# A list scheduler whose machine model is replaced, with 243 instead of 225 score tiles on VectorE

## The chip, the cores and the metric

The kernel runs on one core of one Trainium2 chip. Its engines are TensorE (PE, with its weight loads listed apart as PEld), VectorE (DVE), ScalarE (ACT), GpSimd (POOL) and SyncE (SP). The metric is the device time of one execution in microseconds. The kernel before took 881.84 us, the median of three runs (879.56 to 889.25). One further execution, which took 881.67 us, was recorded by the hardware profiler; all views of the profile are from it.

## The reference

Two attention branches read the same input and are mixed by a gate. All operands are bfloat16; S = 2048 tokens, D = 512, H = 32 heads of 16.

```python
g = sigmoid((x * gate_w).sum(-1, keepdims=True))
# branch A: softmax attention
q, k, v = split(x @ A_wqkv)                     # 32 heads of 16
p = softmax(q @ k.T / 4)                        # 2048 x 2048 for each head
a = (p @ v) @ A_wo
# branch B: linear attention with softmax features
q, k, v = split(x @ B_wqkv)
phi = lambda t: concat(softmax(t @ w_phi), softmax(-t @ w_phi))
num = phi(q) @ (phi(k).T @ v);  den = phi(q) @ phi(k).sum(0)
b = (num / (den + 1e-6)) @ B_wo
out = g * a + (1 - g) * b
```

Nearly all the work is branch A's 32 x 2048 x 2048 exponentials and the two products around them.

## The kernel before

**Tiles.** A score tile is 128 keys by 512 queries of one head: 32 heads x 16 key tiles x 4 query chunks = 2048 tiles. Four heads that share a quarter-wise layout go together, so the tiles are numbered in packs of four (512 packs); an output group is 16 packs (all key tiles of four heads and one query chunk), and there are 32 groups. A score matmul (`_scores`, L792) contracts over 32 rows (two heads of 16, the other head's queries set to zero), and stands in one of four row groups of the array ("row" kind). A value matmul (`_values`, L893) has 32 output columns (the head's 16 values, a column of ones that gives the softmax's sum, and 15 that nobody reads) and stands in one of four column groups ("col" kind). Everything else on TensorE uses the full array ("full" kind).

**Who computes the exponential.** ScalarE takes most tiles. PSUM has eight banks; five form a ring for ScalarE's scores, which are taken in groups of three and two banks in turn: `_qk` issues two or three score matmuls (L792), `_exp` one ACTIVATE over 1536 or 1024 columns (L837) into the SBUF ring ET. The score group k waits for the exponential k - 2, whose banks it reuses. The remaining three banks serve all else. VectorE takes the tiles named in `self.away`: `SHARES` gives for each output group how many of its 64 tiles go there, 225 in all. They are worked in batches of five (`_vector_batch`): a score matmul "vqk" for each into a common bank (also L792), its evacuation to integers (L731), and then on all five together four polynomial steps (L740, L742, L744, L746) and a last one (L748) that makes the bits of a bfloat16 exponential, in tile vu. The value product of such a tile is "pvx", also at L893, which reads vu.

**Filling TensorE.** `_fill` (L900) adds four matmuls with zero weights to the open output bank, one for each column group, which change nothing in the sum but keep the array busy. While no output bank is open (between the last value product of a group and the first of the next), `_qk` can put up to two full matmuls ahead of its scores into a bank that these overwrite (L809, called pads here).

**Other work.** The projections of branch A run ahead of the heads that need them (L582 for K and Q, L640 for V), the query halves are spread by small DMAs from SP (L624), the outputs are transposed and normalised on VectorE (`_norm`: L914 to L930), branch B (`_branch_b`) is put between, with 16 ScalarE exponentials of 2048 columns (L1057), and output projections close each query chunk (L1171 and L1204).

**What sets the order.** Every operation is recorded as an `Op` in `Plan` with its engine, a cost in microseconds, dependencies, a due time (`prio`) and a release position (`rel`). `Plan.order` is a list scheduler: it keeps for each engine the time at which it is free, takes the operation that can start first, and among those that start within 0.02 us the one with the lowest due time. The outcome is a fixed instruction order for each engine; on the chip the engines run these orders and meet at semaphores (`emit`, `_waits`), so the planner's times themselves do not reach the chip. Four parts of this model matter here:

- costs: `c_act`, `c_dve` and constants in the calls; VectorE's are lowered by 0.06 when placed, and `LAT` is added between dependent operations (on VectorE also within the engine);
- TensorE as one resource with a single free time, a cost for each operation and `SWITCH` where the kind changes;
- a limit for other TensorE work while a score group is available, from the 51st score group on: its ready time plus the cost of the exponential that runs, less `AHEAD` = 0.7;
- fills and pads, added where the array's share of the last 3 us is low (`SHARE`, `PAD`).

Constants place the rest: `LEAD`, `VPRIO` and `VREL` say how far ahead VectorE's batches are due, `QDUE` the query projections, `TPRIO` the transposes of finished outputs, `KEEP` the pack from which a bank is reserved for the next output group, `K0`, `SK`, `Q0` and `SQ` branch B.

Of the kernel before, what the change touches and what calls it, by code (L numbers as in the profile page):

```python
# [7 lines left out]
ALU = mybir.AluOpType  # L8
# [32 lines left out]
class Op:  # L41
    def __init__(self, eng, fn, cost, name, prio, rel, kind, lat):
        self.eng, self.fn, self.cost, self.name = eng, fn, cost, name
        self.prio, self.rel, self.kind, self.lat = prio, rel, kind, lat
        self.deps = []
# [16 lines left out]
class Plan:  # L62
# [4 lines left out]
    LAT = {"PE": 0.20, "ACT": 0.16, "DVE": 0.08, "POOL": 0.12, "SP": 2.2}  # L67
    SWITCH = 0.12
    SPAN, SHARE, FILL = 3.0, 0.6, 0.2133
    PAD, PADS, OVER = 0.5, 2, 0.3  # L70
# [9 lines left out]
    def op(self, eng, fn, cost, reads=(), writes=(), deps=(), name="", prio=0.0, rel=-99, kind="full",  # L80
           acquire=None, release=None, lat=None, array=None):
        o = Op(eng, fn, cost, name, prio, rel, kind, self.LAT[eng] if lat is None else lat)
# [27 lines left out]

    def order(self):
# [9 lines left out]
        last_kind = None  # L121
# [3 lines left out]
        seq = {id(o): i for i, o in enumerate(self.ops)}  # L125
        while left:
            best = None
            for e in self.ENGS:
                found, limit = [], 1e9
                for o in avail[e]:  # L130
# [3 lines left out]
                    t = free[e]  # L134
                    for d in o.deps:
                        r = d.end + (d.lat if d.eng != e or e != "PE" else 0.0)
                        if r > t:
                            t = r
                    if o.acquire is not None:
                        if not self._bank_for(o):  # L140
                            continue
                        r = min(b[1] for b in self.free_banks)
                        if r > t:
                            t = r
                    o.ready = t
                    found.append(o)
                    if o.slack is not None:
                        limit = min(limit, t + o.slack)
                for o in found:
                    cost = o.cost + (self.SWITCH if o.kind != last_kind else 0.0)  # L150
                    o.fits = o.slack is not None or o.ready + cost <= limit
                    key = (o.ready, o.prio, seq[id(o)])
                    if o.fits and (best is None or key < best[0]):
                        best = (key, e)
# [7 lines left out]
            for o in avail[e]:  # L162
                if not o.fits:
                    continue
                if o.ready <= t0 + 0.02:
                    key = (o.prio, seq[id(o)])
# [4 lines left out]
            t = max(o.ready, free[e])  # L171
            while e == "PE" and self.open is not None and self.pad:
                f = free["PE"]
                x = Op("PE", self.pad(self.open), self.FILL, "pad", o.prio, -99, "col", 0.2)
                x.start, x.end = f, f + self.FILL + self.SWITCH * (last_kind != "col")
                room = t + self.OVER * (o.kind == "col") - x.end
                have = sum(r[1] for r in recent if r[0] > f - self.SPAN)
                if have >= self.SHARE * self.SPAN or room < 0:
                    break
                last_kind = "col"  # L180
                free["PE"] = x.end
                recent.append((x.start, self.FILL))
                x.array = self.FILL
                queues["PE"].append(x)
            t = max(t, free[e])
            cost = o.cost - (0.06 if e == "DVE" else 0.0)
            if e == "PE" and o.kind != last_kind:
                cost += self.SWITCH
                last_kind = o.kind
            if e == "PE":  # L190
                recent = [r for r in recent if r[0] > t - self.SPAN]
                recent.append((t, o.array))
                low = lambda share: sum(r[1] for r in recent) < share * self.SPAN
                while o.filler > o.filled and low(self.SHARE) or (
                        o.pad and self.open is None and o.filled < self.PADS and low(self.PAD)):
                    o.filled += 1
                    cost += self.FILL
                    recent.append((t, self.FILL))
            o.start, o.end = t, t + cost
            free[e] = o.end  # L200
# [11 lines left out]
            for u in o.users:  # L212
                u.left -= 1
                if not u.left:
                    avail[u.eng].append(u)
# [85 lines left out]
class _Kernel:  # L301
# [5 lines left out]
    AHEAD = 0.7  # L307
    NB, NVU, LEAD = 5, 3, 17
    QDUE, VPRIO, VREL, TPRIO = 20.0, -4.0, 27.0, 11.0
    KEEP = 14  # L310
# [91 lines left out]
    def c_act(n):  # L402
        return 0.089 + n * 0.000812

    @staticmethod
    def c_dve(n):
        return 0.16 + n * 0.00105

    @staticmethod
    def c_pe(n):  # L410
        return 0.004 + n * 0.000417
# [134 lines left out]
    def _x_transpose(self, j, half, bank=None):  # L546
# [4 lines left out]
        for t2 in range(2):  # L551
# [13 lines left out]
            self._bank(job).bitcast(BF16).rearrange("p (t c q) -> p t c q", t=2, c=4)), 0.7,  # L565
# [65 lines left out]
    def _proj_v(self, cp, j):  # L631
# [5 lines left out]
        for tt in range(4):  # L637
# [6 lines left out]
            mm = op("PE", run, 4 * 0.09, reads=[self.b_xT[j], self.b_WA[2][cp > 0]], deps=[mm], name="vproj", prio=due,  # L644
# [6 lines left out]
    def _gate(self):  # L651
# [5 lines left out]
        for qc in range(NQC):  # L657
            job = Job()

            def mm(e, qc=qc, job=job):  # L660
# [8 lines left out]
                self.T1[:, k].rearrange("p b d -> p (b d)"), self._bank(job)), 0.74, deps=[m], name="gate_t",  # L669
# [14 lines left out]
        for j in range(4):  # L684
# [6 lines left out]
    SHARES = (0, 0, 2, 6, 5, 5, 7, 7, 8, 8, 8, 6, 8, 7, 9, 8,  # L691
              10, 6, 8, 7, 8, 7, 8, 6, 9, 8, 9, 6, 8, 9, 11, 11)
# [22 lines left out]
    def _vector_batch(self, number, units, due, step):  # L715
# [10 lines left out]
        for j, u in enumerate(units):  # L726
# [3 lines left out]
                   acquire=job, array=0.0533)  # L730
# [10 lines left out]
           0.16 + n * 0.00053, reads=[b_vt], writes=[b_vf], name="v_frac", prio=prio)  # L741
        op("DVE", lambda e: e.tensor_scalar(flat(vu), flat(vf), CUBE, SQUARE, op0=ALU.mult, op1=ALU.add),  # L742
           0.16 + n * 0.00027, reads=[b_vf], writes=[b_vu], name="v_line", prio=prio)
        op("DVE", lambda e: e.tensor_tensor(flat(vf), flat(vf), flat(vf), ALU.mult), 0.16 + n * 0.00053,  # L744
# [516 lines left out]
```

## Time and profile before

| | |
|---|---|
| three runs | 879.56, 881.84, 889.25 us |
| the profiled execution | 881.67 us |
| its span, first to last instruction | 879.9 us |
| ScalarE busy | 858.1 us (98%) |
| TensorE busy | 819.6 us (93%) |
| VectorE busy | 774.5 us (88%) |
| mean granted TensorE clock | 0.994 |

The span is the time from the first to the last instruction; 1.77 us of the execution lie around it. Busy time of an engine is the union of its instructions' records. A record lasts longer than the engine's spacing between two instructions, because an instruction drains while the next one runs; so the busy time of ScalarE and VectorE contains short waits. Matmul ends are modelled, so TensorE's busy time is an upper figure as well.

### The profile page before, as it was taken

How to read it: one execution, taken by the hardware profiler on the slowest of the kernel's cores; microseconds unless marked ns; L12 is line 12 of the kernel's file. 1: busy time of each engine (PE TensorE's matmuls, PEld its weight loads, DVE VectorE, ACT ScalarE, POOL GpSimd, SP SyncE). 2: the span in 40 equal slices, each digit the busy share in tenths (PEclk: the TensorE clock that was granted, in tenths of full speed). 3: DMA queues.
4: the chain of work that ended last, by engine and by line, in shares of the span. 5: the costliest groups of instructions: out<-in, count | busy, mean ns of one | idle time of the engine just before them, and what ended most of it. 6: DMA issues, size and time to landing. Idle time of an engine off the chain costs nothing.

```text
span 879.9 us, 17614 instructions
## 1 busy us (share of the span) xinstructions
PE 819.6 (93%) x7777; PEld 253.6 (29%) x7777; DVE 774.5 (88%) x1040; ACT 858.1 (98%) x749; POOL 7.3 (1%) x14
## 2 busy tenths in 40 slices
PE   8999999999999999998989989999999999999998
PEld 3333223223222222222223222232322322232222
DVE  4469588898999989899898997989999999899996
ACT  5999999999999999999999999999999999999996
POOL 3000000000000000000000000000000000000000
PEclk9999999999999989999999999999999999999999
DMA  7200000000000000000000000000000000000000
GB/s 240 55 2 1 7 1 3 6 1 7 1 7 2 7 1 1 8 1 7 1 1 8 1 7 19 7 7 1 13 14 9 6 1 7 19 7 8 1 1 25
DMA packets 14700, 11.51 MB, mean 13 GB/s; under 512 B 5536, under 2 KB 14112, under 8 KB 14624
## 3 DMA queue, kind: packets, MB, share of 16 engines
q1 hardware_dynamic: 12752, 9.73, 3.8%
q8 instruction: 61, 1.00, 0.5%
q10 hardware_dynamic: 1872, 0.66, 0.3%
q14 instruction: 15, 0.12, 0.1%
HBM read 6.31 MB, written 2.10 MB: 10 GB/s over the span
## 4 chain that ended last, share of the span: by engine, by line
ACT 88%; PE 8%; DVE 2%; DMA 1%; SPq 0%; issue 0%; ACTq 0%
ACT ET L837 85%; ACT bq L1057 3%; PE ps L792 3%; PE ps L893 1%; PE ps L900 1%; DVE WB L1005 1%; DMA WA<-in_A_wqkv_dram 1%; PE ps L809 1%; PE ps L582 1%; SPq L624 0%; PE ps L662 0%; DMA qT<-qraw 0%; PE ps L1204 0%; PE ps L1171 0%; DVE kT L605 0%
## 5 line engine op out<-in xcount | busy, mean ns | idle before, releaser
L837 ACT ACTIVATE ET<-ps 128x1536 bf16<-128x1536 f32 x729 | 831.6, 1398 | 12.5 <-PE ps L792 11.8
L792 PE MATMUL ps<-qT,kT 32*128 32x512 bf16 x2048 | 332.5, 386 | 47.9 <-ACT ET L837 37.5
L900 PE MATMUL ps<-kT,zero 128*32 128x512 bf16 x2352 | 224.0, 386 | 0.0
L893 PE MATMUL ps<-ET,V 128*32 128x512 bf16 x1823 | 204.5, 385 | 0.0
L792 PEld LDWEIGHTS ps<-qT,kT 32*128 32x128 bf16 x2048 | 81.4, 91 | 351.4 <-ACT ET L837 293.6
L731 DVE TENSOR_SCALAR vt<-ps 128x512 uint32<-128x512 f32 x225 | 150.1, 683 | 28.2 <-PE ps L792 26.8
L748 DVE SCALAR_TENSOR_TENSOR vu<-vt,vu 128x2560 int16<-128x2560 uint32 x45 | 126.7, 2816 | 0.4
L893 PE MATMUL ps<-vu,V 128*32 128x512 bf16 x225 | 86.1, 386 | 0.0
L900 PEld LDWEIGHTS ps<-kT,zero 128*32 128x32 bf16 x2352 | 54.6, 94 | 73.8 <-issue 60.6
L893 PEld LDWEIGHTS ps<-ET,V 128*32 128x32 bf16 x1823 | 54.8, 95 | 64.0 <-issue 42.4
L740 DVE TENSOR_SCALAR vf<-vt 128x2560 f16<-128x2560 uint8 x45 | 66.8, 1485 | 0.2
L744 DVE TENSOR_TENSOR vf<-vf 128x2560 f16<-128x2560 f16 x45 | 66.7, 1481 | 0.3
L746 DVE TENSOR_TENSOR vu<-vu,vf 128x2560 f16<-128x2560 f16 x45 | 66.6, 1480 | 0.2
L582 PE MATMUL ps<-WB,xT 128*128 128x512 bf16 x192 | 55.5, 383 | 0.0
L582 PE MATMUL ps<-xT,WA 128*128 128x512 bf16 (+1 forms) x132 | 37.1, 380 | 0.5 <-DVE xT L563 0.3
L742 DVE TENSOR_SCALAR vu<-vf 128x2560 f16<-128x2560 f16 x45 | 36.7, 816 | 0.2
L1057 ACT ACTIVATE bq<-bq 128x2048 bf16<-128x2048 bf16 x16 | 33.6, 2100 | 0.0
L893 PEld LDWEIGHTS ps<-vu,V 128*32 128x32 bf16 x225 | 21.4, 95 | 29.9 <-issue 24.8
L914 DVE STREAM_TRANSPOSE T<-ps 128x512 f32<-128x512 f32 x32 | 22.8, 712 | 8.0 <-PE ps L893 7.9
L1032 DVE CAST bq<-ps 128x512 bf16<-128x512 f32 x32 | 21.5, 684 | 6.9 <-PE ps L582 6.9
L640 PE MATMUL ps<-WA,xT 128*128 128x128 bf16 x256 | 21.4, 221 | 1.3 <-DMA WA<-in_A_wqkv_dram 1.2
L1054 DVE TENSOR_TENSOR bq<-bq,btree 128x2048 bf16<-128x2048 bf16 x16 | 19.5, 1221 | 0.2
(84 smaller groups left out, 438.9 us busy)
## 6 DMA issues: line engine op xcount, KB each, us to landing
qT<-qraw SPq DMA_DIRECT2D x120, 16.0 KB, 1.8
xn<-in_A_x_dram SPq DMA_DIRECT2D x3, 512.0 KB, 7.7
WB<-in_B_wqkv_dram SPq DMA_DIRECT2D x1, 1536.0 KB, 8.2
out_dram<-WB SPq DMA_DIRECT2D x12, 128.0 KB, 1.7
WA<-in_A_wqkv_dram SPq DMA_DIRECT2D x3, 384.0 KB, 8.9
xn<-in_A_x_dram SPq DMA_DIRECT2D x2, 256.0 KB, 3.9
wphi<-in_B_w_phi_dram SPq DMA_DIRECT2D x32, 0.5 KB, 1.9
WoA<-in_A_wo_dram SPq DMA_DIRECT2D x1, 512.0 KB, 4.4
```

The lines of the kernel that those rows point to most:

```text
L582: ins = e.matmul(self._bank(job)[:, 0:n], lhs(c), rhs(c), start=(c == 0), stop=(c == 3))
L731: parts.append(op("DVE", lambda e, j=j, job=job: e.tensor_scalar(vt[:, j, :], self._bank(job), SCALE * LOG2E * 2.0 ** 24, 2.0 ** 31, op0=A ...
L740: op("DVE", lambda e: e.tensor_scalar(flat(vf), frac, 1 / 256, ROOT, op0=ALU.mult, op1=ALU.add), 0.16 + n * 0.00053, reads=[b_vt], writes= ...
L742: op("DVE", lambda e: e.tensor_scalar(flat(vu), flat(vf), CUBE, SQUARE, op0=ALU.mult, op1=ALU.add), 0.16 + n * 0.00027, reads=[b_vf], writ ...
L744: op("DVE", lambda e: e.tensor_tensor(flat(vf), flat(vf), flat(vf), ALU.mult), 0.16 + n * 0.00053, reads=[b_vf], writes=[b_vf], name="v_sq ...
L746: op("DVE", lambda e: e.tensor_tensor(flat(vu), flat(vu), flat(vf), ALU.mult), 0.16 + n * 0.00053, reads=[b_vf, b_vu], writes=[b_vu], name ...
L748: o = op("DVE", lambda e: e.scalar_tensor_tensor(out=flat(vu).bitcast(I16), in0=flat(vt), scalar=2.0 ** -17, in1=flat(vu), op0=ALU.mult, o ...
L792: return e.matmul(out, self.kT[32 * i:32 * i + 32, cp, kt * TOK:(kt + 1) * TOK], self.qT[32 * i:32 * i + 32, s, :], start=True, stop=True, ...
L837: o = plan.op("ACT", lambda e: e.activation(self.ET[:, a % NS:a % NS + n, :], self.ps[:, a % NR:a % NR + n, :], ACT.Exp, scale=SCALE), sel ...
L893: ins = e.matmul(self._bank(ot)[32 * i:32 * i + 32, :], self.V[:, kt, g8 // 2, v0:v0 + 32], tile, start=(kt == 0), stop=(kt == self.NT - 1 ...
L900: ins = e.matmul(self._bank(ot)[32 * i:32 * i + 32, :], self.zero[:], self.kT[:, 0, 0:QCH], start=False, stop=False, tile_position=(0, 32 ...
L1057: op("ACT", lambda e: e.activation(flat, flat, ACT.Exp), self.c_act(2048) + 0.2, reads=[b], writes=[b], name="b_exp", prio=due + 1)
```

## The change

The planner's model of the machine is replaced, and the shares and due times that go with it.

- TensorE is kept as four column or row groups. An operation names the groups that it uses; each is held for 0.2133 us, the next matmul may start 0.003 later, and a change of kind waits for all groups and 0.104 more (`_place`).
- Costs and latencies are other numbers: `c_act`, `c_dve`, `c_pe` and the single costs. The flat 0.06 taken off VectorE's costs goes, and so does the latency between dependent operations of one engine.
- The limit for other TensorE work holds from the third score group on and is tied to the end of the running exponential, less 0.435. A fill has to meet it too.
- Free matmuls (fills) are put ahead of an operation as long as they delay it by no more than a bound; `PAD` is -0.4, so the full pads of `_qk` no longer come.
- `SHARES` gives 243 tiles to VectorE: 48 batches of five and one of three.
- `LEAD`, `QDUE`, `VPRIO`, `VREL`, `TPRIO`, `KEEP`, `K0`, `Q0` and `SQ` have other values.

All computation is as before, apart from which engine takes a tile. Lines move by 30: L731 becomes L761, L792 L822, L837 L867, L893 L923, L900 L930.

```diff
-    LAT = {"PE": 0.20, "ACT": 0.16, "DVE": 0.08, "POOL": 0.12, "SP": 2.2}
-    SWITCH = 0.12
+    LAT = {"PE": 0.21, "ACT": 0.333, "DVE": 0.138, "POOL": 0.12, "SP": 2.2}
+    WIDE, NEXT, SWITCH = 0.2133, 0.003, 0.104
     SPAN, SHARE, FILL = 3.0, 0.6, 0.2133
-    PAD, PADS, OVER = 0.5, 2, 0.3
+    PAD, PADS, OVER = -0.4, 2, 0.25
+    ALL = (0, 1, 2, 3)
+    AHEAD = 0.0
...
+    def _place(self, state, kind, groups, cost, t):
+
+        last_kind, busy, last = state
+        t = max(t, last)
+        if kind != last_kind:
+            t = max(t, max(busy) + self.SWITCH)
+        if groups is None:
+            t = max(t, max(busy))
+            return t, t + cost, (kind, (t + cost,) * 4, t + cost)
+        b, first = list(busy), None
+        for g in groups:
+            t = max(t, b[g])
+            first = t if first is None else first
+            b[g] = t + self.WIDE
+            t += self.NEXT
+        return first, max(b[g] for g in groups), (kind, tuple(b), t)
...
                     if o.slack is not None:
-                        limit = min(limit, t + o.slack)
+                        due = t if o.slack.end is None else o.slack.end - 0.435 - self.AHEAD
+                        limit = min(limit, max(t, due))
...
-                    o.fits = o.slack is not None or o.ready + cost <= limit
+                    o.fits = o.slack is not None or limit > 1e8 or o.last + self.SWITCH * (o.kind != "row") <= limit
...
-            t = max(o.ready, free[e])
-            while e == "PE" and self.open is not None and self.pad:
...
+                t = max(o.dep_t, o.ready if o.acquire is not None else 0.0)
+                while self.open is not None and self.pad:
+                    first, end, state = self._place(pe, "col", self.ALL, 0, 0.0)
+                    have = sum(r[1] for r in recent if r[0] > max(first, o.ready - self.FILL) - self.SPAN)
+                    room = self._place(state, o.kind, o.groups, o.cost, t)[0] - o.ready
+                    if have >= self.SHARE * self.SPAN or room > self.OVER * (o.kind == "col"):
+                        break
+                    if room > 0 and pe_limit < self._place(state, o.kind, o.groups, o.cost, t)[1] + self.SWITCH:
+                        break
...
-                while o.filler > o.filled and low(self.SHARE) or (
+                while (o.filler > o.filled and low(self.SHARE) and end + self.FILL + self.SWITCH <= pe_limit) or (
                         o.pad and self.open is None and o.filled < self.PADS and low(self.PAD)):
...
-            cost = o.cost - (0.06 if e == "DVE" else 0.0)
...
+                t = o.end + (o.lat if u.eng != e or o.name.startswith("dma") else 0.0)
...
-    AHEAD = 0.7
-    NB, NVU, LEAD = 5, 3, 17
-    QDUE, VPRIO, VREL, TPRIO = 20.0, -4.0, 27.0, 11.0
-    KEEP = 14
+    NB, NVU, LEAD = 5, 3, 21
+    QDUE, VPRIO, VREL, TPRIO = 24.0, -14.0, 43.0, 6.0
+    KEEP = 13
...
     def c_act(n):
-        return 0.089 + n * 0.000812
+        return 0.052 + n * 0.000832
...
     def c_dve(n):
-        return 0.16 + n * 0.00105
+        return 0.065 + n * 0.001047
...
-    SHARES = (0, 0, 2, 6, 5, 5, 7, 7, 8, 8, 8, 6, 8, 7, 9, 8,
-              10, 6, 8, 7, 8, 7, 8, 6, 9, 8, 9, 6, 8, 9, 11, 11)
+    SHARES = (0, 0, 2, 7, 7, 4, 7, 6, 7, 8, 9, 7, 8, 7, 13, 6,
+              11, 8, 9, 6, 7, 9, 10, 10, 7, 7, 9, 4, 12, 12, 10, 14)
...
-           0.16 + n * 0.00053, reads=[b_vt], writes=[b_vf], name="v_frac", prio=prio)
+           0.057 + n * 0.000525, reads=[b_vt], writes=[b_vf], name="v_frac", prio=prio)
...
         o.pad = k >= 8
-        if k >= 50:
-            o.slack = self.exps[k - 1].cost - self.AHEAD
+        if k >= 2:
+            o.slack = self.exps[k - 1]
...
-    K0, SK, Q0, SQ = 25.0, 12.0, 212.0, 16.5
+    K0, SK, Q0, SQ = 29.0, 12.0, 200.0, 17.75
```

## The prediction

> **What bounds the kernel now.** I read the chain that ended last first, then the groups of instructions, then windows, waits and single stretches of the timeline.
>
> ```profile
> ACT 88%; PE 8%; DVE 2%; DMA 1%; SPq 0%; issue 0%; ACTq 0%
> ...
> L837 ACT ACTIVATE ET<-ps 128x1536 bf16<-128x1536 f32 x729 | 831.6, 1398 | 12.5 <-PE ps L792 11.8
> ...
> L900 PE MATMUL ps<-kT,zero 128*32 128x512 bf16 x2352 | 224.0, 386 | 0.0
> ...
> L731 DVE TENSOR_SCALAR vt<-ps 128x512 uint32<-128x512 f32 x225 | 150.1, 683 | 28.2 <-PE ps L792 26.8
> L748 DVE SCALAR_TENSOR_TENSOR vu<-vt,vu 128x2560 int16<-128x2560 uint32 x45 | 126.7, 2816 | 0.4
> ```
>
> The chain is ScalarE's exponential (L837) for nearly its whole length. The page shows it idle for only 12.5 us, 7 of them before its first instruction, so it looks full. The same rows split by shape show that it is not:
>
> ```profile
> L837 ACT ACTIVATE ET<-ps 128x1536 bf16<-128x1536 f32 x365 | 586.8, 1608 | 11.4 <-PE ps L792 11.0
> L837 ACT ACTIVATE ET<-ps 128x1024 bf16<-128x1024 f32 x364 | 432.2, 1187 | 1.1 <-PE ps L792 0.8
> ```
>
> The durations add up to 1019 us inside 831.6 us of busy time: each record overlaps the next, so a short stall hides under the previous record. Start to start, the undisturbed spacing is 1.330 us after a 1536-wide exponential and 0.903 after a 1024-wide one. 365 x 1.330 + 364 x 0.903 = 814.1 us of need. Against this need the starts are late by 18.2 us in sum between first and last exponential. I sorted these stalls by what stood ahead of the late score group on TensorE: 3.7 us lie in two stretches at half clock, 2.1 behind the L809 pad matmuls at full clock, 2.6 before 65 us (score groups without a deadline), 7.2 with other TensorE work or a TensorE wait for VectorE ahead, and 2.6 in pieces under 0.04 us.
>
> ```profile
> 320.00:330.00 10.00, 9.63 (x68) 1.99 (x68) 7.44 (x14) 8.48 (x8) 0.00 (x0) 0.66 0.00 0
> 455.00:460.00 5.00, 4.98 (x29) 1.17 (x29) 3.76 (x10) 3.51 (x4) 0.00 (x0) 0.66 0.00 0
> 120.00:840.00 720.00, 675.39 (x6510) 202.04 (x6503) 663.76 (x886) 715.89 (x625) 0.00 (x0) 0.99 0.02 6
> ```
>
> Columns: stretch, length, busy PE, PEld, DVE, ACT, POOL, granted clock. In the first two the clock averages 0.66 and ScalarE loses 1.5 us each. The third is the body: VectorE is busy 663.8 of 720 us, idle 56.2. Nearly half of that is one wait in the body, for the scores of its own tiles:
>
> ```profile
> DVE vt L731 <- PE ps L792: 23.8, 41, 2.5
> ```
>
> **The change part by part.** The base is the profiled execution: 881.67 us, span 879.9, 1.77 outside it; the median of the runs, 881.84, is 0.17 above.
>
> *Tiles moved off ScalarE.* 18 more tiles go to VectorE; the built order has 361 + 361 exponentials for 365 + 364. Four wide and three narrow go: 4 x 1.330 + 3 x 0.903 = **-8.0 us**, all on the chain. The busy time gives the same (831.6 / 1823 x 18 = 8.2).
>
> *Tiles moved onto VectorE.* L731, L740 (66.8 us), L742 (36.7), L744 (66.7), L746 (66.6) and L748 sum to 513.6 us for 225 tiles, 2.283 each; 18 cost 41.1 us, and VectorE goes from 774.5 to 815.6 busy. By SHARES, 15 of the 18 fall in output groups 5 to 31, so the body takes 663.8 + 15 x 2.283 = 698.0. It lies beside ScalarE and costs nothing while VectorE waits less: that cover is the 56.2 us idle. The old costs bear on it: L731 was planned at 0.16 + 512 x 0.00105 - 0.06 = 0.638 us, with 0.08 more before a dependent one; start to start the trace has 0.601. The new 0.065 + 512 x 0.001047 is 0.601. The old plan thus took VectorE for some 8% fuller than it was, and 243/225 is 8% more: the idle time was the plan's error, and the new plan spends it.
>
> *TensorE.* Score and value products stay at 2048 each. Fills (L900) go from 2352 to 2688: 84 sets of four, one 0.213 us start to start, +17.9 us. The 21 pads go (-4.5), and changes between row-, column- and full-array kinds fall from 1622 to 1483; one costs 0.104 (score group to next fill 0.32 less 0.213), -14.5. The sum is -1 us, on an engine 93% busy, so where work stands matters. Counting in both built orders the work between score groups two apart at these prices (groups on distinct quarters side by side), it exceeds the 2.23 us of a wide plus a narrow exponential 208 times before and 145 times after. I scale the 7.2 us of stalls behind other work by 145/208, to 5.0: **-2.2 us**. Bounds: all gone (-7.2) and none gone.
>
> *Pads gone* (PAD is negative): their stalls at full clock go, **-2.1 us**; the next late thing there is the score group's own release. What they covered is below.
>
> *Deadlines from the third score group on, not the 51st, and tied to the exponential's end less 0.435 us.* I let half of the 2.6 us of early stalls go: **-1.3 us** (bounds 0 and -2.6). Later groups get no more room: the lowest spacing from a last score matmul to its exponential is 0.43 us, 131 exponentials already stand within 0.03 of it, and the new margin is 0.435 less 0.423 (0.213 for the matmul, 0.21 to ScalarE).
>
> *Start.* The built order puts all 16 V projections ahead of the first score group, where 8 stood:
>
> ```profile
> 9.63 0.62 PE L640 MATMUL ps<-WA,xT 128*128 128x128 bf16 x8 [1.17 <-DMA WA<-in_A_wqkv_dram]
> 10.18 0.39 PE L792 MATMUL ps<-qT,kT 32*128 32x512 bf16 x3
> ```
>
> Eight take 0.44 us after a DMA that is late anyway, and nothing hides them: **+0.4 us**. The 16 transposes now behind that group (0.9 us) lie under a 1.33 us exponential.
>
> *Due times and KEEP.* Projections, norms and bank reservations move by a few positions. SP issues the same DMAs; eight query loads fall behind the first stores, whose queue is nearly empty. The nearest rows are TensorE waits for query loads (1.5 us) and VectorE waits for value sums (L914, 7.9 us, beside ScalarE): between -1.5 and, if such a wait reaches the chain, +8. I take 0, nearest the first row.
>
> *Sum.* The half-clock stretches (3.7) and the small pieces (2.6) stay. -8.0 - 2.2 - 2.1 - 1.3 + 0.4 = -13.2, or **868.5 us**.
>
> **The rivals.**
>
> *VectorE becomes the bound (slower).* The body shrinks to about 720 - 15 x 0.446 (ScalarE's time for a tile) - 3 = 710 us, so VectorE's idle time there must fall from 56.2 to 12 us. Each microsecond above 12 lengthens the run by one, since late VectorE tiles close output groups late and TensorE, in order, holds the next scores behind them. If 36 us stay (64% of today's) the time is 868.5 + 24 = **892.5**; it passes 890.5 (1% slower) from 34. For it: the 23.8 us behind L792, which needs a PSUM bank that VectorE itself frees. Against it: those waits arose because VectorE ran ahead of an overrated plan.
>
> *The clock.* TensorE cannot fill while no output bank is open:
>
> ```profile
> 455.02 0.94 PE L809 MATMUL ps<-kT 128*128 128x512 bf16 x2 [1.83 <-ACT ET L837]
> ...
> 456.55 1.45 ACT L837 ACTIVATE ET<-ps 128x1536 bf16<-128x1536 f32 x1 [0.67 <-PE ps L792]
> ```
>
> TensorE idles 1.83 us, pads stand behind the wait and cover nothing, and the clock halves. Now no pads exist at all, and at two group changes the built order leaves 4.0 and 3.1 us of ScalarE work (a 1.8 us softmax exponential inside each) with 0.37 and 0.21 us of full-array work. One half-clock stretch cost 3.7 / 2 = 1.85 us; five more give **878**. The Trainium skill, "TensorE: Matmul & The Clock Gate", section "Why this matters for your kernels", allows no idle gap over about 3 us, else half rate. By that rule two gaps qualify, +3.7 us on the sum, 872.2; the trace agrees in kind but is stricter, with 1.83 us of idle inside a thin stretch.
>
> *No margin, so only the work moves.* Both loaded engines are planned to the nanosecond, and new small stalls replace the old: 881.67 - 8.0 + 0.4 = **874**. That is also the case in which the scheduler doesn't do what it says. For it: the 131 groups without slack, which carry 12.0 of the 18.2 us.
>
> *The plan holds.* Stalls fall to 5 us: 874 - 13.2 = **861**. For it: the new constants meet the trace's spacings (0.052 + 1536 x 0.000832 = 1.330).
>
> **How the numbers follow.** Forecast (864 to 872) 0.45; plan holds 0.15; no margin 0.18; clock 0.10; VectorE 0.12, of which 0.02 stays under 890.5. The range 860 to 882 leaves out the slow VectorE cases and the best of "holds". Within 1% (about what a measurement of this kernel can tell) is 873.0 to 890.5. Faster: 0.45 + 0.15 + 0.02 of the no-margin case = 0.62; slower 0.10; same 0.28.
>
> **What would show it.** Exponentials: 722, some 823 us busy. VectorE near 816 us busy, about 12 us idle in the body: 30 or more means the VectorE rival, with ScalarE's gaps ending behind VectorE-released scores. Stalls by start spacing: 12.6 in sum; 5 means the plan holds, 18 no margin. More than two half-clock stretches, at group changes, mean the clock. First exponential at 11.06 us for 10.62. The prediction is wrong as a whole if VectorE's tiles overtake ScalarE on the chain.

## The result and the profile after

The changed kernel takes 919.25 us (median of four runs, 914.47 to 921.75), the kernel before in the same comparison 882.70 (four runs). The ratio is 1.040, with a 95% interval of 1.032 to 1.047: slower by 4%, where 868.5 us and a range of 860 to 882 had been predicted. The profiled execution took 920.96 us.

The page of the kernel after: its span, the busy time of each engine, the chain that ended last, and the groups that answer to the lines shown of before.

```profile
span 919.2 us, 18274 instructions
...
PE 829.9 (90%) x8092; PEld 254.9 (28%) x8092; DVE 830.1 (90%) x1078; ACT 858.7 (93%) x742; POOL 7.3 (1%) x14
...
DVE 70%; PE 14%; ACT 10%; SPq 3%; issue 2%; DMA 1%; ACTq 0%
...
L867 ACT ACTIVATE ET<-ps 128x1536 bf16<-128x1536 f32 x722 | 828.1, 1293 | 47.1 <-PE ps L822 45.5
...
L930 PE MATMUL ps<-kT,zero 128*32 128x512 bf16 x2688 | 243.6, 398 | 0.0
...
L761 DVE TENSOR_SCALAR vt<-ps 128x512 uint32<-128x512 f32 x243 | 158.8, 682 | 27.9 <-PE ps L822 27.3
L778 DVE SCALAR_TENSOR_TENSOR vu<-vt,vu 128x2560 int16<-128x2560 uint32 (+1 forms) x49 | 137.0, 2796 | 0.6
```

The chain has changed hands: ScalarE's 88% before are 10% now, and VectorE has 70%. The mean granted clock fell from 0.994 to 0.965. The same exponentials by shape, and then the body in the view by windows (stretch, length, busy PE, PEld, DVE, ACT, POOL, granted clock):

```profile
L867 ACT ACTIVATE ET<-ps 128x1536 bf16<-128x1536 f32 x361 | 543.8, 1506 | 25.9 <-PE ps L822 25.0
L867 ACT ACTIVATE ET<-ps 128x1024 bf16<-128x1024 f32 x361 | 389.7, 1080 | 21.3 <-PE ps L822 20.4
```

```profile
120.00:840.00 720.00, 650.89 (x6375) 192.64 (x6373) 680.76 (x878) 684.52 (x589) 0.00 (x0) 0.96 0.02 6
```

ScalarE waits openly 45.5 us for scores where it waited 11.8. In the same 720 us of body it is busy 684.5 us (715.9 before), and VectorE 680.8 with 39.2 us idle.

Where the 39.3 us between the two spans (879.9 and 919.2) come from, by the starts of the exponentials:

| us | before | after |
|---|---|---|
| first exponential starts | 10.62 | 9.68 |
| from first to last start | 859.8 | 900.0 |
| of these: need at the undisturbed spacings 1.330 and 0.903 | 814.1 | 806.1 |
| of these: stalls | 18.0 | 65.8 |
| last start to the end of the span | 9.4 | 9.4 |
| stretches at half clock, in sum | 10.3 | 66.4 |

The rest of the time from first to last start, some 28 us in both, goes to the 16 softmax exponentials of branch B and the small one of the gate. Of the 66.4 us at half clock 1.5 lie after the last instruction.

The need fell by the 8.0 us that were forecast, and the stalls grew by 47.8. Of the 65.8 us of stalls some 30 stand in stretches at half clock. Another 26 or so stand behind a TensorE wait or other TensorE work at full clock; 14 to 19 of these are behind a wait for VectorE, by how far back from the late score group one looks. The rest are pieces under 0.04 us and softmax exponentials that start late.

**What is slow.** VectorE's instructions have the shapes and single durations of before, yet their busy time is 830.1 us where 815.6 was worked out. The difference is in the spacing. From the timeline of the kernel after, VectorE alone (start, duration, line, operation, output from input):

```profile
313.87 0.71 DVE L944 STREAM_TRANSPOSE T<-ps 128x512 f32<-128x512 f32 x1
314.62 0.21 DVE L951 TENSOR_TENSOR rinv<-T,gh 128x32 f32<-128x32 f32 x1
...
317.43 1.49 DVE L774 TENSOR_TENSOR vf<-vf 128x2560 f16<-128x2560 f16 x1
318.84 0.68 DVE L761 TENSOR_SCALAR vt<-ps 128x512 uint32<-128x512 f32 x1
319.44 1.48 DVE L776 TENSOR_TENSOR vu<-vu,vf 128x2560 f16<-128x2560 f16 x1
320.95 2.83 DVE L778 SCALAR_TENSOR_TENSOR vu<-vt,vu 128x2560 int16<-128x2560 uint32 x1
```

L761 does not need what L774 made, and starts 1.41 us after L774, while that record still runs. L778 reads the tile vu that L776 has just written, and starts 1.51 us after it, behind the record's end. Both front instructions take 1.48 to 1.49 us by themselves. Sorted in this way, whether the next instruction needs the result of the one in front of it, the medians are:

| start to start, us | next one independent | next one dependent |
|---|---|---|
| L776 (before: L746) | 1.40 | 1.52 |
| L774 (L744) | 1.40 | 1.52 |
| L772 (L742) | 0.733 | 0.853 |
| L761 (L731) | 0.600 | 0.717 |
| L944 (L914) | 0.633 | 0.744 |
| L1100, the reciprocal of branch B | 0.87 | 0.99 |

A dependent neighbour costs 0.11 to 0.13 us more, on long and short instructions alike. The order of before has 102 such neighbours among 1040 VectorE instructions; the order of after has **350 among 1078**. All 350 cost 350 x 0.12 = 42 us; the 248 that before does not have cost 30 us.

The planner's latency rule decides this. Before, it added 0.08 us between dependent VectorE operations, so that the start of a dependent one was later than that of any other that was ready, and the list scheduler put the other one between. After, the next step of a chain is ready at the same instant as everything else, and chains are run off in one go.

### The profile page after: what moved, and what is told of

It reads as the page before. It is cut to its first block, busy times and chain, and to the rows that moved or that the text cites. A ratio compares the mean times of both kernels' runs of the same rounds, so it can differ in the third digit from the quotient of the medians.

```text
span 919.2 us, 18274 instructions
## 1 busy us (share of the span) xinstructions
PE 829.9 (90%) x8092; PEld 254.9 (28%) x8092; DVE 830.1 (90%) x1078; ACT 858.7 (93%) x742; POOL 7.3 (1%) x14
## 4 chain that ended last, share of the span: by engine, by line
DVE 70%; PE 14%; ACT 10%; SPq 3%; issue 2%; DMA 1%; ACTq 0%
DVE vt L761 11%; DVE vu L778 11%; ACT ET L867 10%; DVE vf L774 6%; DVE vu L776 6%; DVE vf L770 5%; PE ps L822 5%; DVE vu L772 3%; SPq L654 3%; PE ps L930 3%; PE ps L923 2%; DVE bq L1084 2%; DVE bq L1062 2%; DVE bq L1094 2%; DVE T L944 2%
## 5 line engine op out<-in xcount | busy, mean ns | idle before, releaser
L867 ACT ACTIVATE ET<-ps 128x1536 bf16<-128x1536 f32 x722 | 828.1, 1293 | 47.1 <-PE ps L822 45.5
L822 PE MATMUL ps<-qT,kT 32*128 32x512 bf16 x2048 | 335.7, 396 | 64.9 <-ACT ET L867 27.8
L930 PE MATMUL ps<-kT,zero 128*32 128x512 bf16 x2688 | 243.6, 398 | 0.0
L923 PE MATMUL ps<-ET,V 128*32 128x512 bf16 x1805 | 199.9, 394 | 4.3 <-DVE T L944 2.2
L761 DVE TENSOR_SCALAR vt<-ps 128x512 uint32<-128x512 f32 x243 | 158.8, 682 | 27.9 <-PE ps L822 27.3
L822 PEld LDWEIGHTS ps<-qT,kT 32*128 32x128 bf16 x2048 | 80.4, 91 | 360.0 <-ACT ET L867 205.8
L778 DVE SCALAR_TENSOR_TENSOR vu<-vt,vu 128x2560 int16<-128x2560 uint32 (+1 forms) x49 | 137.0, 2796 | 0.6
L923 PE MATMUL ps<-vu,V 128*32 128x512 bf16 x243 | 92.1, 394 | 1.9 <-DVE vu L778 1.8
L930 PEld LDWEIGHTS ps<-kT,zero 128*32 128x32 bf16 x2688 | 61.7, 95 | 113.0 <-issue 96.2
L774 DVE TENSOR_TENSOR vf<-vf 128x2560 f16<-128x2560 f16 (+1 forms) x49 | 72.2, 1474 | 0.7
L776 DVE TENSOR_TENSOR vu<-vu,vf 128x2560 f16<-128x2560 f16 (+1 forms) x49 | 72.2, 1473 | 0.6
L770 DVE TENSOR_SCALAR vf<-vt 128x2560 f16<-128x2560 uint8 (+1 forms) x49 | 72.2, 1473 | 0.2
L923 PEld LDWEIGHTS ps<-ET,V 128*32 128x32 bf16 x1805 | 52.7, 96 | 62.7 <-issue 31.6
L772 DVE TENSOR_SCALAR vu<-vf 128x2560 f16<-128x2560 f16 (+1 forms) x49 | 39.8, 813 | 0.2
L944 DVE STREAM_TRANSPOSE T<-ps 128x512 f32<-128x512 f32 x32 | 22.7, 709 | 4.4 <-PE ps L923 4.4
L923 PEld LDWEIGHTS ps<-vu,V 128*32 128x32 bf16 x243 | 22.7, 97 | 12.9 <-issue 7.2
L635 DVE CAST kT<-ps 128x512 bf16<-128x512 f32 x15 | 10.3, 690 | 12.3 <-PE ps L612 12.3
```

The costliest lines, as they stand in the source:

```text
L761: parts.append(op("DVE", lambda e, j=j, job=job: e.tensor_scalar(vt[:, j, :], self._bank(job), SCALE * LOG2E * 2.0 ** 24, 2.0 ** 31, op0=A ...
L770: op("DVE", lambda e: e.tensor_scalar(flat(vf), frac, 1 / 256, ROOT, op0=ALU.mult, op1=ALU.add), 0.057 + n * 0.000525, reads=[b_vt], write ...
L776: op("DVE", lambda e: e.tensor_tensor(flat(vu), flat(vu), flat(vf), ALU.mult), 0.057 + n * 0.000525, reads=[b_vf, b_vu], writes=[b_vu], na ...
L778: o = op("DVE", lambda e: e.scalar_tensor_tensor(out=flat(vu).bitcast(I16), in0=flat(vt), scalar=2.0 ** -17, in1=flat(vu), op0=ALU.mult, o ...
L822: return e.matmul(out, self.kT[32 * i:32 * i + 32, cp, kt * TOK:(kt + 1) * TOK], self.qT[32 * i:32 * i + 32, s, :], start=True, stop=True, ...
L867: o = plan.op("ACT", lambda e: e.activation(self.ET[:, a % NS:a % NS + n, :], self.ps[:, a % NR:a % NR + n, :], ACT.Exp, scale=SCALE), sel ...
```

## The experiments

Theories: T1, the missing latency between dependent VectorE operations, by the order that it makes. T2, VectorE is too full with 243 tiles. T3, the clock, because no pads are left. T4, the planner gives score groups and query loads no margin. In the table "pairs" counts neighbours on VectorE of which the second needs the first. Each ratio is against the runs of before taken in the same comparison (medians from 880.63 to 882.70 us), with its 95% interval.

| run | pairs | time, us | ratio to before | stalls | half clock |
|---|---|---|---|---|---|
| before | 102 | 882.70 | 1 | 18.0 | 10.3 |
| after | 350 | 919.25 | 1.040 | 65.8 | 66.4 |
| e1_gate8 | 365 | 915.06 | 1.038 (1.032 to 1.044) | 57.1 | 71.7 |
| e2_latency | 86 | 877.51 | 0.995 (0.993 to 0.998) | 17.3 | 16.9 |
| e3_pads | 354 | 916.52 | 1.040 (1.034 to 1.046) | 59.8 | 52.2 |
| e4_shares225 | 359 | 920.34 | 1.044 (1.039 to 1.050) | 55.2 | 69.0 |
| e7_before_nolat | 343 | 894.97 | 1.015 (1.008 to 1.022) | 32.5 | 23.1 |
| e12_latency04 | 112 | 879.20 | 0.997 (0.993 to 1.001) | 20.5 | 18.4 |
| e13_latency02 | 349 | 904.52 | 1.026 (1.020 to 1.031) | 43.6 | 39.2 |
| e5_margin_load | 70 | 883.48 | 1.001 (0.997 to 1.004) | 18.9 | 23.2 |
| e6_margin_load_225 | 110 | 889.63 | 1.008 (1.005 to 1.010) | 23.5 | 38.1 |
| e8_nolat_margin_load | 354 | 925.80 | 1.049 (1.041 to 1.057) | 60.3 | 65.6 |
| e9_shares238 | 80 | 872.80 | 0.989 (0.984 to 0.994) | 15.0 | 20.4 |
| e10_shares237 | 83 | 880.56 | 0.997 (0.994 to 1.000) | 18.6 | 40.6 |

Stalls and half clock are from the one profiled execution of each, and up to 2.7 us of the half clock lie after the last instruction.

**A control.** With a VectorE latency in the planner, the gate's projection (four full matmuls kept together) finds no place between score groups at its old due time. e1 moves that due time alone:

```diff
-            m = op("PE", mm, 4 * self.c_pe(512), reads=[self.b_xT[qc], b_gwb], name="gate", prio=18 + qc, rel=12,
+            m = op("PE", mm, 4 * self.c_pe(512), reads=[self.b_xT[qc], b_gwb], name="gate", prio=8 + qc, rel=12,
```

> The changed kernel with the gate's due time at 8 instead of 18 and nothing else: a control for the next run, which needs this edit. All theories: as the changed kernel, 910 to 926 us, some 350 VectorE instructions right behind their producers, half clock for 30 to 80 us.

It stays at 915.06 us. The due time of the gate is not the cause, and e1 is the base for the next one.

**The latency back, in the new model.**

```diff
-                t = o.end + (o.lat if u.eng != e or o.name.startswith("dma") else 0.0)
+                t = o.end + (o.lat if u.eng != e or o.name.startswith("dma") else 0.12 if e == "DVE" else 0.0)
```

> The control with one more edit: the planner counts 0.12 us between dependent operations on VectorE again (the change had dropped it; in the trace of the changed kernel 350 of 1078 VectorE instructions stand right behind their producer and cost 0.117 to 0.13 us more there, 42 us in sum, against 102 of 1040 before). 243 tiles stay on VectorE. Theory 1, the dropped latency overloads VectorE and all else follows: about 100 such pairs, VectorE's waits gone with them, 860 to 880 us. Theory 2, 243 tiles are too many: 900 us or more. Theory 3, the missing pads let the clock fall: 900 us or more, half clock still over 50 us.

It takes 877.51 us, 37.6 less than e1, with the same 243 tiles and still no pads. Its page, the body in the view by windows, and VectorE's timeline where the same output transpose stands:

```profile
span 874.0 us, 18208 instructions
...
PE 807.0 (92%) x8060; PEld 251.7 (29%) x8060; DVE 805.3 (92%) x1078; ACT 848.0 (97%) x742; POOL 7.3 (1%) x14
...
ACT 91%; PE 4%; SPq 4%; issue 0%; DVE 0%; DMA 0%; ACTq 0%
```

```profile
120.00:840.00 720.00, 666.14 (x6783) 199.15 (x6781) 691.69 (x918) 716.39 (x627) 0.00 (x0) 0.99 0.02 6
```

```profile
296.54 0.71 DVE L944 STREAM_TRANSPOSE T<-ps 128x512 f32<-128x512 f32 x1
297.17 0.25 DVE L1092 TENSOR_TENSOR bsum<-btree 128x128 f32<-128x128 f16 x1
297.34 0.20 DVE L951 TENSOR_TENSOR rinv<-T,gh 128x32 f32<-128x32 f32 x1
297.46 0.95 DVE L1100 RECIPROCAL brec<-bsum 128x128 f16<-128x128 f32 x1
298.32 0.30 DVE L953 RECIPROCAL rinv<-rinv 128x32 f32<-128x32 f32 x1
```

The norm's chain (L944, L951, L953) and branch B's (L1092, L1100) now alternate, and L944 is followed after 0.63 us, not 0.75. The same 1078 instructions are busy 805.3 us instead of 830.1: 24.8 us less for 264 fewer pairs, 0.09 each. That is about the overlap of records that a dependent neighbour loses (0.083 in the median; the other 0.03 is idle time behind the record). ScalarE has the chain back, and VectorE has only 28.3 us idle in the body. So VectorE can carry 243 tiles: T2 falls.

**The pads back, without the latency.**

```diff
-    PAD, PADS, OVER = -0.4, 2, 0.25
+    PAD, PADS, OVER = 0.5, 2, 0.25
```

> The changed kernel with PAD back at 0.5, so that full matmuls can fill while no output bank is open. Theory 3 (clock): half clock under 20 us and 880 to 895 us. Theories 1 and 2: 908 us or more, since the clock falls because TensorE waits for VectorE.

916.52 us, the same ratio as after, with 34 pads in the trace where before had 21 and after none. Half clock falls from 66.4 to 52.2 us and the time does not follow. T3 as a cause falls; e2, with no pads, has 16.9 us at half clock.

**Fewer tiles, without the latency.**

```diff
-    SHARES = (0, 0, 2, 7, 7, 4, 7, 6, 7, 8, 9, 7, 8, 7, 13, 6,
-              11, 8, 9, 6, 7, 9, 10, 10, 7, 7, 9, 4, 12, 12, 10, 14)
+    SHARES = (0, 0, 2, 6, 5, 5, 7, 7, 8, 8, 8, 6, 8, 7, 9, 8,
+              10, 6, 8, 7, 8, 7, 8, 6, 9, 8, 9, 6, 8, 9, 11, 11)
```

> The changed kernel with the old SHARES, 225 tiles on VectorE. VectorE needs 18 x 2.28 = 41 us less, ScalarE 8 us more. Theory 2 (too many tiles): 882 us or less. Theory 1: the 42 us of dropped latency are still unplanned, VectorE is still late against the plan and everything else waits for it at the wrong places: 885 to 900 us, about 350 pairs. Theory 3: 905 us or more.

A miss for T1 and T2: 920.34 us, no gain at all. The figure lies in the range given to T3, but half clock is 69.0 us, much as in after, and e2 and e3 speak against the pads. Its page:

```profile
PE 832.5 (91%) x8204; PEld 257.3 (28%) x8204; DVE 793.8 (86%) x1040; ACT 863.9 (94%) x749; POOL 7.3 (1%) x14
...
DVE 55%; ACT 23%; PE 14%; SPq 3%; DMA 2%; issue 2%; ACTq 0%; DVEq 0%
```

VectorE is idle 61.8 us in the body, more than in the kernel before, and is still most of the chain. A VectorE with more time to spare did not cure this order. That its results come late at the places where TensorE, in its own order, waits for them, and its idle time at others, fits this but is not shown. Why 225 tiles cost just as much as 243 here is not settled; one wait of 16.2 us of the output transpose (L944) for the value products stands out.

**The latency out of the kernel before**, whose costs, shares, deadlines and pads all stay:

```diff
-                        r = d.end + (d.lat if d.eng != e or e != "PE" else 0.0)
+                        r = d.end + (d.lat if d.eng != e else 0.0)
```

> The kernel before with one edit: its planner, too, counts nothing between dependent VectorE operations. Its order then has 343 instructions right behind their producers for 102, 241 x 0.12 = 29 us more on VectorE; against that its costs stay too high by 0.037 us for each of 1040 (38 us). Theory 1 (the dropped latency hurts where the costs leave no reserve): slower, but by less than the changed kernel is, 885 to 900 us. Theory 2 (tiles) and theory 3 (pads, which this kernel has): 878 to 885, no change.

894.97 us, inside T1's range and 1.5% over before. The edit drops the latency on ScalarE, GpSimd and SyncE as well, but the order that it builds is the same, operation for operation, as with VectorE's alone dropped. The pairs go from 102 to 343 and VectorE's busy time from 774.5 to 791.8 us:

```profile
PE 817.7 (91%) x7841; PEld 258.5 (29%) x7901; DVE 791.8 (88%) x1040; ACT 860.9 (96%) x749; POOL 7.3 (1%) x14
```

One edit to the old planner reproduces the effect, at about 14 us for 241 pairs, less than half of what the new one pays. The old planner's VectorE costs were higher than the trace's spacing (0.638 planned for 0.601) and its limit for other TensorE work 0.7 us earlier; that this slack took up the rest is argued, not shown.

**Is it the planned length or the order?** A latency of 0.04 is a third of the real one, so the planned times stay too short, but it is above the 0.02 us within which the scheduler goes by due times alone. 0.02 is not.

```diff
-                t = o.end + (o.lat if u.eng != e or o.name.startswith("dma") else 0.0)
+                t = o.end + (o.lat if u.eng != e or o.name.startswith("dma") else 0.04 if e == "DVE" else 0.0)
```

> The control (changed kernel, gate due at 8) with 0.04 us between dependent VectorE operations, a third of what they take. It is enough for the scheduler to prefer another operation: 112 instructions right behind their producer in the built order for 365. If it is the order that costs (the pairs), 875 to 885 us. If it is the planned length of VectorE's chains, a third of the gain of 0.12: 900 us or more.

> The same with 0.02 us, which falls within the 0.02 us in which the scheduler takes the lowest due time: the built order keeps 349 pairs. Order: 905 us or more. Planned length: a sixth of the gain, about 908.

With 0.04 the pairs fall to 112 and the time to 879.20 us; with 0.02 they stay at 349 and it takes 904.52. A third of the latency in the plan brings 35.9 of the 37.6 us that 0.12 brings, so the length in the plan matters little, and the time goes with the number of pairs. The two forecasts for e13 (905 or more, and about 908) lie too close for it to tell them apart by itself. It beats e1 by 10.5 us at nearly the same number of pairs (349 for 365). Only the order reaches the chip, so something else in the order matters too; what, is open.

**Margins.** T4 on top of T1: score groups planned with 0.04 us to spare, query loads at the 0.58 us that the trace has for one issue (0.589 median) in place of 0.45, and the gate in two halves. e5 has the latency of e2, e6 has 225 tiles besides, e8 lacks the latency.

```diff
-    AHEAD = 0.0
+    AHEAD = 0.04
...
-        o = self.plan.op("SP", parts, 0.45 * len(parts), reads=[self.b_qraw[n % 2]], writes=[self.b_qT[s0]],
+        o = self.plan.op("SP", parts, 0.58 * len(parts), reads=[self.b_qraw[n % 2]], writes=[self.b_qT[s0]],
...
+            for hf in range(2):
...
+                m = op("PE", mm, 2 * self.c_pe(512), reads=[self.b_xT[qc], b_gwb], deps=[m], name="gate",
+                       prio=18 + qc, rel=12, acquire=None if hf else job)
```

> The changed kernel with four edits to the planner: 0.12 us between dependent VectorE operations, the gate's matmuls as two operations of two (so that they fit the windows; no due time is touched), a margin of 0.04 us on the score deadline, and 0.58 instead of 0.45 us for each of a query load's eight DMAs (6.2 to 7.7 us were measured from evacuation to landing for 5.8 planned). 243 tiles. The run with the latency alone loses 0.4 to 0.5 us in each 40 us to pieces of some 0.02 us, and 4 us before its 40th us, behind a query load. If those come from the missing margin and the load, they go: 862 to 872 us. If they are jitter that no margin meets: 875 to 880.

> The same with 225 tiles. If VectorE can carry 243 tiles once its latency is planned, ScalarE's eight microseconds come back: 8 us slower than the run with 243 (870 to 882). If 243 tiles crowd VectorE, this one is faster than that.

> The first kernel of this set without the latency: gate in two, margin and loads only. Theory 1: 900 us or more, some 350 pairs and half clock over 40 us, since margin and loads don't touch the cause. If the tight deadlines or the late loads were the cause: under 885 us.

e5 is a miss: 883.48 us, in neither range and not under e2. Its stalls are 18.9 us, so the margin brought nothing that shows. In the profiled executions it loses 1.9 us against e2 by its 26th exponential and 3.0 us after the start of the last one (15.4 for 12.4), where ScalarE waits 10.7 us for the output projections (7.6 in e2). e6 lies above its range (870 to 882), as e5 does, and is 6.2 us slower than e5: that is what the 18 tiles are worth in this order, against the 8.0 forecast. e8 differs from e5 in the latency alone and takes 925.80 us, 42.3 more. That is the cleanest pair of the study: T4 does not cure what T1 causes, and the latency is worth 42 us in this plan, for 284 pairs. In after, TensorE's matmuls wait 9.8 us for query loads where before had 0.9, which looked like a cause of its own; with the loads planned at their measured length and the latency missing, nothing is won.

**Better than both?** e9 takes the latency, the gate in two halves, SP's DMA issues at costs from the trace, no margin, KEEP 14, and 238 tiles with fewer in the last groups. Two of these edits:

```diff
-    KEEP = 13
+    KEEP = 14
...
-    SHARES = (0, 0, 2, 7, 7, 4, 7, 6, 7, 8, 9, 7, 8, 7, 13, 6,
-              11, 8, 9, 6, 7, 9, 10, 10, 7, 7, 9, 4, 12, 12, 10, 14)
+    SHARES = (0, 0, 2, 7, 7, 4, 7, 6, 7, 8, 9, 8, 8, 7, 13, 6, 11, 8, 9, 6, 7, 9, 10, 10, 8, 7, 9, 4, 12, 10, 10, 9)
```

> The same without a margin, VREL 43 and 238 tiles, 41 of them in the last four groups. As the run before it: 862 to 872 us, or 874 to 882 if start and end are not what it loses.

> An attempt at a faster kernel on what the runs showed: 0.12 us between dependent VectorE operations, the gate in two operations, a margin of 0.02 us, DMA issue costs on SP as the trace has them (0.58 us for a query load's part, 0.53 and 0.8 for the small loads, 1.5 for the large weights), VREL 27 and KEEP 14 as before, and 237 tiles with 42 instead of 48 in the last four output groups, since the run with 243 and the latency ends 12.5 us after the start of its last exponential, the kernel before 9.4. If start and end were what the 243 tiles cost: 862 to 872 us. If not: 874 to 882.

e9 takes 872.80 us, ratio 0.989 (0.984 to 0.994), the fastest kernel of the study and 1.1% under before. It lies between the two ranges given. Its page:

```profile
span 870.7 us, 18127 instructions
...
PE 800.0 (92%) x7994; PEld 253.0 (29%) x8052; DVE 793.4 (91%) x1068; ACT 850.9 (98%) x744; POOL 7.3 (1%) x14
...
ACT 93%; PE 5%; DVE 1%; issue 0%; ACTq 0%
```

e2 and e9 both run 851.5 us from first to last exponential; e9 then ends 9.2 us after the last one starts, e2 12.4, since 16 output matmuls stand ahead of its last value products. e10 (237 tiles, a margin of 0.02, VREL 27, other last groups) had been expected near e9; it took 880.56, in the second range, with 40.6 us at half clock. Which of its differences matters was not tried. Several knobs went together in e9, so the run shows that such a plan exists and not which knob made it.

## Why the prediction was wrong

**The step that failed** is "Tiles moved onto VectorE", at "The old costs bear on it". It put the cost of the added VectorE work on the time at nothing, since it "lies beside ScalarE". The prediction read 0.601 us as L731's spacing, set it against the planned 0.638 "with 0.08 more before a dependent one", and concluded that "the idle time was the plan's error, and the new plan spends it". The 0.601 is the median over all neighbours, and in the order of before nine in ten neighbours are independent, because the 0.08 was in the plan. The term was thus sized on the outcome of the very rule that the change removes. The "some 8%" hides the same slip: by the cost formulas alone a batch of five was planned at 11.14 us before and is at 10.69 now, which is 4%; the only other item that the sentence names is the latency, and that was no error. What the runs showed in its place is that dropping the latency costs 37.6 us (e2 against e1) to 42.3 us (e5 against e8). The 102 dependent pairs were in the trace of before too, 12 of them behind L746. From its timeline, an independent neighbour of L746 (1.40 us later) and then a dependent one (1.52 us later):

```profile
308.71 1.49 DVE L746 TENSOR_TENSOR vu<-vu,vf 128x2560 f16<-128x2560 f16 x1
310.11 0.69 DVE L1051 TENSOR_TENSOR btree<-bq 128x1024 bf16<-128x1024 bf16 x1
...
86.96 1.48 DVE L746 TENSOR_TENSOR vu<-vu,vf 128x2560 f16<-128x2560 f16 x1
88.48 2.83 DVE L748 SCALAR_TENSOR_TENSOR vu<-vt,vu 128x2560 int16<-128x2560 uint32 x1
```

The 12 dependent ones have a median of 1.517. That split, made before the forecast, would have given 0.12 us a pair; the built order of after, with 350 pairs, was there to be counted. The true latency is more than the 0.08 that looked too high.

The Trainium skill, "VectorE: DVE Perf Modes", section "The DRAIN you can't avoid", says that eight copies take 13.88 us with a semaphore after each or only after the last, so that "the semaphore costs nothing extra here". This case measures otherwise where the semaphore guards a result that the next instruction needs: 0.12 us more than for a neighbour that needs nothing from it. The measurement decides here.

**From the pairs to the time.** VectorE's chains end later than the plan has them, and TensorE, in order, waits for a VectorE result with score groups behind it. One case from the timeline of after (the bracket gives the idle time and what ended it):

```profile
400.63 0.39 PE L822 MATMUL ps<-qT,kT 32*128 32x512 bf16 x2
...
401.70 0.71 DVE L944 STREAM_TRANSPOSE T<-ps 128x512 f32<-128x512 f32 x1
...
402.47 0.40 PE L923 MATMUL ps<-ET,V 128*32 128x512 bf16 x4 [1.45 <-DVE T L944]
...
403.28 0.39 PE L822 MATMUL ps<-qT,kT 32*128 32x512 bf16 x3
...
403.72 1.45 ACT L867 ACTIVATE ET<-ps 128x1536 bf16<-128x1536 f32 x1 [0.88 <-PE ps L822]
```

The value products need the bank that the transpose L944 empties; TensorE idles 1.45 us, and the exponential behind the next scores is 0.88 us late. Soon after, the clock halves; the stretch in the view by windows:

```profile
404.20:421.30 17.10, 17.07 (x122) 3.80 (x118) 13.46 (x18) 12.23 (x11) 0.00 (x0) 0.50 0.00 1
```

At 0.50 of full clock TensorE is busy throughout, and ScalarE has work for 12.2 of 17.1 us. Of nine such stretches eight follow a TensorE wait of 1.0 to 1.65 us by less than 4 us: five waits for VectorE, two for query loads, one for an exponential. The ninth, from 35.6 us on, falls into a wait of 4.12 us for a query load:

```profile
36.14 0.60 PE L822 MATMUL ps<-qT,kT 32*128 32x512 bf16 x1 [4.12 <-DMA qT<-qraw]
```

Such a wait does not decide alone: seven others of 1.1 to 1.55 us in the same trace, four of them for VectorE's results, are followed by no half clock.

So most of the slower clock stands behind TensorE's waits for VectorE, and a part behind other waits. The sizes do not add up simply. The 248 more pairs are 30 us of VectorE's time, and the stalls grew by 47.8 us. The half-clock stretches, with some 30 us of stalls for 3.7 before, can hold the difference, but how much the clock adds by itself no run separates. The step from the dropped latency to the pairs and to the time is shown by the runs; the way through TensorE's waits and the clock is read from the trace.

**The other terms.**

- *Tiles moved off ScalarE, -8.0*: the need fell by just that, and e5 against e6 gives 6.2 us in time.
- *TensorE -2.2, pads -2.1, deadlines -1.3*: the stalls should have fallen to 12.6 us. In e2, with the spacing cured, they are 17.3 for 18.0 before. In that order the three together are worth under 1 us; which of them failed was not separated. About half of e2's exponentials start 0.01 to 0.03 us late, as the "no margin" rival had it, and its price (874) is nearer to e2's 877.5 than the forecast is.
- *Start, +0.4*: the first exponential came 0.94 us earlier, not 0.44 later. The weight load that it stands behind landed at 8.19 us, for 9.58 before. From that landing to the first exponential it is 1.49 us in after and in e1, for 1.04 before: the term was right, and an earlier landing hid it. In e1, where the load lands at 9.53, the first exponential starts at 11.02, for the 11.06 forecast.
- *Due times, 0*: after ends as before did, 9.4 us behind the start of its last exponential. In e2, with the same due times but for the gate, this tail is 3 us longer.

**The rivals.** "VectorE becomes the bound", at a chance of 0.12, had the right sign, the right engine and the right way to the end (TensorE holds the next scores behind VectorE), and its mark, 30 us or more of VectorE idle in the body, was met with 39.2. Its price of 892.5 fell 27 us short: it counted idle time that VectorE could not use, while most of the lost spacing shows as busy time in the records, and it left out the clock. Idle time was also the wrong gauge: e4 leaves 61.8 us idle and is no faster, e2 28.3 and beats before. "The clock" came as well, 66.4 us at half rate, but mostly behind VectorE and not for want of pads (e3, e2). The rule cited there from the Trainium skill, "TensorE: Matmul & The Clock Gate", section "Why this matters for your kernels" (no idle gap over about 3 us), fits the stretch at 35.6 us (4.12 us idle) and is too lenient for the other eight, whose waits are 1.65 us at most. "The plan holds" is met by no run.

## What to carry to other kernels

Before a scheduler's latency is called an error, split the trace's spacings by whether the next instruction needs the one in front: a median over all of them is close to the value of whichever kind the present order prefers. A list scheduler puts independent work between dependent steps only if its model says that waiting costs something; here 0.04 us in the plan was enough to win most of the 0.12 on the chip. And when engines run fixed orders, a late engine does damage with idle time left: look at who waits for it, not only at how full it is (here e4 left VectorE 61.8 us idle and was no faster).

## What the runs showed of the hardware

- A VectorE instruction that needs the result of the one right in front of it starts 0.11 to 0.13 us later than an independent one, whether the first takes 0.14 or 1.40 us start to start. A record of an independent neighbour overlaps the one before by 0.083 us in the median, and a dependent one starts 0.034 us behind it, so VectorE's busy time changes by reordering alone (805.3 us in e2, 830.1 in after, for the same 1078 instructions).
- In after TensorE's clock halved nine times, for 3.4 to 17 us at a time: eight times within 4 us of a single TensorE wait of 1.0 to 1.65 us, once inside one of 4.12 us. Seven waits of 1.1 to 1.55 us in the same trace, and one of 1.86 us in before, were followed by none, so the length of one wait does not decide it.
- One 16 KB query load takes 0.589 us of SP's time to issue; a set of eight takes 4.9 to 6.4 us, and TensorE's matmuls waited for such loads seven times in after (9.8 us) and twice before (0.9 us).
